# Four pairs of weight slices in seven products for the second batch, and where a fifth pair's weight sums are made

## The chip, the cores and the metric

The kernel runs on one core of a Trainium2 chip. The metric is the device time of one execution in microseconds (us). Three runs of the kernel before gave 648.67, 646.83 and 647.27 us, so a median of 647.27 us.

## The reference

Two stages are computed for 4 batches of 768 tokens. The first is attention of 8 heads of width 64 over chunks of 32 tokens (with 16 tokens of context on the left, 8 on the right and 8 memory tokens). The second is a mixer over the result `x`, cut here to what matters:

```python
h = x.transpose(0, 2, 1) @ U @ V              # over tokens, rank 32
u = x + h.transpose(0, 2, 1)                  # 768 x 512 per batch
ch = np.maximum(u @ w_ch1, 0.0) @ w_ch2       # 512 -> 2048 -> 512
return (u + ch).astype(np.float32)
```

Nearly all of TensorE's time goes into the two products of the last but one line. The kernel keeps each factor of them as a high and a low part (`h` and `l` at the end of a name) and a product is three passes: high by high, low by high, high by low.

## The kernel before

The 2048 hidden columns are 16 slices of 128, numbered f, in 8 pairs p = 0 to 7 (f = 2p and 2p+1). The 768 tokens of a batch are two blocks of 384 (three tiles of 128).

**Batch 0** (`both_blocks`, L1566) works in 32 units. A unit is one slice for one block: `w1_step` (12 matmuls of 384 columns into a PSUM bank `ps_h`), relu and split into `hh` and `hl`, then `w2_step` (9 matmuls of 512 columns into three accumulators). The second block takes its last slices in the order 15, 14, 10, 11, 12, 13, so the last unit, n = 31, is slice 13.

**Batches 1 to 3** (`sevens`, L1304) take a pair of slices and both blocks together. The four products of half slices by half blocks' channels that would be eight are made as seven from sums of weights and sums of `u` (a Strassen form). A product is `six` (L1311): 6 matmuls of 384 columns. The seven run in the order 0 to 6 in the loop from L1399, with copies (`keep`, ScalarE) and additions (`add`, VectorE) of partial results between them. Product 2 and product 4 use the same bank, so product 4 starts only after `keep(c12, xb)`; products 4 and 5 read the sums `t34h`, `t34l` of `u`.

**In batch 1** the first `2 * NPL` = 10 slices (`few`) don't go that way. In the loop at L1374 each slice is two products with the plain weights (`half_of`, `other`), for the first block; its second block follows after the loop over pairs (`other_half`, two products a slice). So five pairs take eight products each (L1355, L1360, L1449) and pairs 5, 6 and 7 take seven.

**Sums of weights.** The sums that products 2, 3, 4 and 6 need are made once per pair, in `take_value` (L511) and `keep_sums` (L487). GpSimd adds high and low part of a slice (`whole`, L485) and makes four sums (L495); ScalarE and VectorE split each into high and low (L498, L499); `save_sums` (L502) writes them to DRAM with four DMAs. The working place is `vbs[1]` (two halves of it are also the home of the first two sums) and two slots, so one pair must be finished with before the next one begins. Pairs 7, 5 and 6 are done at the end of batch 0, pairs 0 to 3 in the loop of L1374, and pair 4 behind `other_half` of slices 8 and 9. The saves of one pair are issued when the next one is taken.

**The ring of weights.** Low parts and sums come from DRAM in items of 256 KB, in the order of `list_items` (L1270), into a ring of 5 tiles `w1l`; `next_item` (L1299) gives out one and asks for the item four ahead. Loads wait for the tile that they overwrite: for the matmuls that read it and, in the plain slices, for `whole` on GpSimd.

**What sets the order.** TensorE and the DMA queue of SyncE (SP) run in the order of the program text. VectorE, ScalarE and GpSimd are ordered by a list scheduler when the kernel is built, except that ScalarE and VectorE keep the text's order among the instructions emitted between L1384 (the last plain slice) and `closing.close()` (L1421, behind the first pair's first split). The attention of the next batch (`attention`, L526) is a generator of 49 pieces, handed out by `pace` (L1648): after call t of `give`, `49 * t // slots` pieces have been emitted. `slots` (L1675) is 47. Piece 14 is `s_part(0)`, the scores of one third of the tokens (L708) with their maximum, subtraction, exponent and sums (L715 to L744); 25 and 33 are the same for the other thirds; 16 and 17 transpose the first third's probabilities (L762), and 19 is `av_part(0)` (L782). The sums of `u` for batch 1 (`seven_u`, L1193) are handed out by `NEXTS` in the last three plain slices; what is left of them, `t34h` and `t34l`, is emitted behind the first pair's first split (L1416).

```python
        product(xb, 0, True)                      # L1408
        ...
        keep(c11, xb)
        even()
        product(yb, 1, True)
        add(c11, yb, c11)
        h1 = split(c11)
        ...
        product(xb, 2, False)                     # L1423
        keep(c12, xb)
        give()
        product(yb, 3, True)
        other_places()
        product(xb, 4, False)
```

In batch 1 `even` and `give` hand out pieces of attention, and `other_places` does nothing. Between the two parts of the quotation, for the first pair alone, lie the rest of `seven_u`, the `w2_step` of the last plain slice and `closing.close()`.

Of the kernel before, what the change touches and what calls it, by code (L numbers as in the profile page):

```python
# [35 lines left out]
SPLIT = 10  # L36
# [5 lines left out]
PACE = 27  # L42
NSOLO = 2
SEVEN = 1
NPL = 5
LASTW = 13
NEXTS = {3: (1, 1), 2: (2, 3), 1: (1, 1)}
RING = 4
# [12 lines left out]
def chunk_attn_then_mixer_kernel(  # L61
# [56 lines left out]
    def w1_home(f, shape, dtype, name):  # L118
        return (w1q if f >= LASTW else w1r if f in (2 * NPL - 2, 2 * NPL - 1) else w1p).tile(shape, dtype, name=name, tag=f"w1_{f}")

# [245 lines left out]
    def save_w1l():  # L366
        while unsaved:
            f, w1l = unsaved.pop(0)
            p, odd = divmod(f, 2)
            for n, w in enumerate((w1h[f], w1l)):  # L370
                if odd:
                    nc.sync.dma_start(out=w1s_d[p][:, 5, n].bitcast(F32), in_=w[:, 2:4].bitcast(F32))
                    if n or p < NPL:
                        nc.sync.dma_start(out=w1x_d[p][:, n].bitcast(F32), in_=w[:, 0:2].bitcast(F32))
# [87 lines left out]
    def advance(n):  # L462
        for _ in range(n):
            next(weights, None)
# [7 lines left out]
    def load_w1l(f, w1l):  # L472
        p, odd = divmod(f, 2)
        if odd:
            nc.sync.dma_start(out=w1l[:, 0:2].bitcast(F32), in_=w1x_d[p][:, 1].bitcast(F32))
            nc.sync.dma_start(out=w1l[:, 2:4].bitcast(F32), in_=w1s_d[p][:, 5, 1].bitcast(F32))
        else:
            nc.sync.dma_start(
                out=w1l.bitcast(F32).rearrange("p (i c) n -> p i c n", i=2), in_=w1s_d[p][:, 0:2, 1].bitcast(F32),
            )  # L480
# [3 lines left out]
    def whole(out, hi, lo):  # L484
        nc.gpsimd.tensor_tensor(out=out, in0=hi.bitcast(F32), in1=lo.bitcast(F32), op=ALU.add)  # L485

    def keep_sums(p, even, odd, homes):  # L487

        half = 2 * P
        a11, a12, a21, a22 = even[:, :half], even[:, half:], odd[:, :half], odd[:, half:]  # L490
        for out, in0, in1, op in (
            (a22, a21, a22, ALU.add), (a21, a11, a21, ALU.subtract),
            (a11, a22, a11, ALU.subtract), (a12, a12, a11, ALU.subtract),
        ):
            nc.gpsimd.tensor_tensor(out=out, in0=in0, in1=in1, op=op)  # L495
        for (i, val), pair in zip(((3, a22), (4, a21), (2, a11), (6, a12)), homes):
            hi, lo = (pair.bitcast(F32R)[:, half * n:half * n + half] for n in range(2))
            nc.scalar.copy(out=hi, in_=val)  # L498
            nc.vector.tensor_tensor(out=lo, in0=val, in1=hi.bitcast(F32), op=ALU.subtract)  # L499
            unkept.append((p, i, pair))  # L500

    def save_sums():  # L502
        for p, i, pair in unkept:
            nc.sync.dma_start(
                out=w1s_d[p][:, i].rearrange("p h c n -> p (h c n)").bitcast(F32), in_=pair.bitcast(F32),
            )
        unkept.clear()
# [3 lines left out]
    def take_value(f, w1l, homes):  # L511

        p, odd = divmod(f, 2)
        values[f] = homes(f % 2)
        whole(values[f], *(w.rearrange("p c n -> p (c n)") for w in (w1h[f], w1l)))
        if 2 * p in values and 2 * p + 1 in values:
            save_sums()
            keep_sums(p, values.pop(2 * p), values.pop(2 * p + 1), [homes(2 + n) for n in range(4)])
# [604 lines left out]
    def more_w():  # L1123
        while loaded[0] < min(NF, done[0] // 2 + EARLY):
            if loaded[0] >= 5 and front[0]:
                return
            if loaded[0] >= LASTF - NDEC and done[0] < ndec[0]:
                return
            load_w(loaded[0])
            loaded[0] += 1  # L1130
# [32 lines left out]
    def turn_x1(c):  # L1163

        ps = att_ps()
        for tt in range(TB):
            nc.tensor.matmul(
                out=ps[:, tt * P:(tt + 1) * P], lhsT=xs[(0, TB + tt)][:, c * P:(c + 1) * P],
                rhs=ident, start=(tt == 0), stop=False, skip_group_check=True,
            )  # L1170
        return ps
# [93 lines left out]
    ring, fetched, used, items = [], [0], [0], []  # L1265

    def others(few):
        return list(range(few - 2, few)) + list(range(few - 2)) if few else []

    def list_items(b):  # L1270

        def whole_item(src):
            def load(w):
                nc.sync.dma_start(
                    out=w.rearrange("p h c n -> p (h c n)").bitcast(F32),
                    in_=src.rearrange("p h c n -> p (h c n)").bitcast(F32),
                )

            return load

        def low_item(f):
            return lambda w: load_w1l(f, w.rearrange("p i c n -> p (i c) n"))

        few = 2 * NPL if b == 1 else 0
        items.extend(low_item(f) for f in range(few))
        items.extend(whole_item(w1s_d[p][:, n]) for p in range(few // 2, NF // 2) for n in range(7))
        for f in others(few):
            p, odd = divmod(f, 2)
            items.append(whole_item(w1x_d[p] if odd else w1s_d[p][:, 0]))
            items.append(whole_item(w1s_d[p][:, 5 if odd else 1]))  # L1290

    def fetch_sums(upto):
        while fetched[0] < min(len(items), upto):
            w = wlo.tile([P, 2, 2, P], F32R, name="w1l")
            items[fetched[0]](w)
            ring.append(w)
            fetched[0] += 1
# [6 lines left out]
    def sevens(b, give, following, last_step=None):  # L1304

        few, closing = 2 * NPL if b == 1 else 0, ExitStack()
        if few:
# [254 lines left out]
    def get_w1l(f):  # L1562
        if f not in w1ls:
            w1ls[f] = fetch_w1l(f)

    def both_blocks():  # L1566

        units = []
        for f in range(SPLIT + LEAD):
            if f < SPLIT:  # L1570
                units.append((0, f, 0, f == 0, None))
            if f >= LEAD:
                g = f - LEAD
                units.append((1, g, 1, g == 0, False if g == SPLIT - 1 else None))
        units += [(0, f, 0, False, True if f == NF - 1 else None) for f in range(SPLIT, NF)]
        order = [NF - 1, NF - 2] + list(range(SPLIT, NF - 2))
        units += [(1, f, 0, f == order[0], True if f == order[-1] else None) for f in order]
        prev, taken = None, [0]
        for n, (blk, f, where, begins, ends) in enumerate(units):
            while done[0] < min(2 * NF, 2 * f + 2):  # L1580
                advance(1)
                more_w()
            if n == 2:
                head.close()
            if n == PACE:
                paced.close()
            for _ in range(SPREAD.get(n, 0)):
                next(spreading)
            for blk_, m, *_ in units[n:n + AHEAD + 3]:
                if SPLIT <= m < NF - 2 and blk_ == 1:  # L1590
                    get_w1l(m)
            if n + RING >= len(units):
                if not items:
                    list_items(1)
                fetch_sums(n + RING + 1 - len(units))
            w1l = w1ls[f]
            if SPLIT <= f < NF - 2 or blk == 1:
                del w1ls[f]
            placed = iter(PLACE.get(n, ()))

            def between():
                upto = next(placed, 0)
                while taken[0] < upto:
                    next(gen[0])
                    taken[0] += 1

            def joins():
                for c, g3 in rest:
                    join_uT1(turn_x1(c), c, g3)
                advance(2)  # L1610

            hid_ = w1_step(0, blk, f, w1l, between if n else joins)
            if blk and f >= 2 * NPL:
                take_value(f, w1l, slot_home if f >= NF - 2 else work_home)
            for _ in range(RATE):
                if n >= 2 * SPLIT or done[0] < 2 * (f + WLO):
                    advance(1)
                more_w()
            between()
            if prev is not None:  # L1620
                while done[0] < 2 * prev[1] + 2:
                    advance(1)
                    more_w()
                w2_step(0, *prev, between)
            between()
            prev = (blk, f, where, begins, ends) + hid_
        return lambda: w2_step(0, *prev)
# [43 lines left out]

    gen[0], coming[0] = attention(1, xs), seven_u(1, fine=True)
    last_step = both_blocks()
    for b in range(1, B):
        slots = 2 * 2 * NPL - 1 + 6 * (NF // 2 - NPL) + 2 + 2 * LATER if b == 1 else 6 * (NF // 2) + LATER  # L1675
        if b == 1:
# [37 lines left out]
```

## Time and profile before

| | before |
|---|---|
| median of three runs | 647.27 us (646.83 to 648.67) |
| the profiled execution, its own time | 647.38 us |
| its span, first to last instruction | 645.6 us |
| TensorE matmul busy | 622.4 us, 96% |
| VectorE, ScalarE, GpSimd busy | 375.4, 255.5, 113.9 us |
| mean granted TensorE clock | 0.994 |

The span starts at 0. Batch 0's last `w2_step` ends at 218.4 us, where batch 1's first product starts; its plain slices run until 265.0 us, its three pairs until 312.4 us, and batch 2 starts at about 373 us. A row of the timeline gives start, duration, engine, line, operation and operands, and in brackets how long the engine stood idle before it and what ended that. Matmuls overlap, so a row's duration is not what a matmul costs: the distance from one row's start to the next one's is.

### The profile page before, as it was taken

How to read it: one execution, taken by the hardware profiler on the slowest of the kernel's cores; microseconds unless marked ns; L12 is line 12 of the kernel's file. 1: busy time of each engine (PE TensorE's matmuls, PEld its weight loads, DVE VectorE, ACT ScalarE, POOL GpSimd, SP SyncE). 2: the span in 40 equal slices, each digit the busy share in tenths (PEclk: the TensorE clock that was granted, in tenths of full speed). 3: DMA queues.
4: the chain of work that ended last, by engine and by line, in shares of the span. 5: the costliest groups of instructions: out<-in, count | busy, mean ns of one | idle time of the engine just before them, and what ended most of it. 6: DMA issues, size and time to landing. Idle time of an engine off the chain costs nothing.

```text
span 645.6 us, 15062 instructions
## 1 busy us (share of the span) xinstructions
PE 622.4 (96%) x6027; PEld 538.6 (83%) x6030; DVE 375.4 (58%) x715; ACT 255.5 (40%) x641; POOL 113.9 (18%) x202
## 2 busy tenths in 40 slices
PE   8788999999899999999999999999999999999997
PEld 5657999988786888788889799998977899999886
DVE  6947788798783837844655835553456732222323
ACT  4525444448332545522255613421347621221221
POOL 4200000043154455100434100000025200000000
PEclk9899999999999999999999999999999999999999
DMA  8994577667897699666489859667423055565201
GB/s 235 170 351 169 178 247 225 229 190 179 179 183 203 158 320 284 198 183 186 140 242 204 164 166 308 202 169 196 119 70 94 1 183 176 147 174 153 97 0 50
DMA packets 168706, 115.03 MB, mean 178 GB/s; under 512 B 100956, under 2 KB 139484, under 8 KB 168636
## 3 DMA queue, kind: packets, MB, share of 16 engines
q1 hardware_dynamic: 168012, 113.92, 63.0%
q8 instruction: 48, 0.79, 0.5%
q10 hardware_dynamic: 624, 0.15, 0.1%
q14 instruction: 22, 0.18, 0.1%
HBM read 90.83 MB, written 28.97 MB: 186 GB/s over the span
## 4 chain that ended last, share of the span: by engine, by line
PE 57%; DVE 5%; ACT 3%; DMA 3%; issue 2%; SPq 1%; POOL 1%; ACTq 0%
PE ps_h L1315 24%; PE acc L1546 16%; PE acc L1556 8%; PE ps_a L782 2%; PE ps_h L1495 2%; ACT uc L171 1%; DMA blocks<-spread 1%; PE acc L1540 1%; DMA w1l<-w1s 1%; SPq L610 1%; PE ps_a L708 1%; PE ps_a L812 1%; PE ps_a L762 1%; DVE x L1511 1%; POOL vb L495 1%
## 5 line engine op out<-in xcount | busy, mean ns | idle before, releaser
L1546 PE MATMUL acc<-w,hh 128*128 128x512 f32 x612 | 157.7, 393 | 1.3 <-ACT hh L1329 1.3
L1546 PEld LDWEIGHTS acc<-w,hh 128*128 128x128 f32 x612 | 113.3, 188 | 22.9 <-ACT hh L1329 2.8
L1556 PE MATMUL acc<-w,hl 128*128 128x512 f32 x306 | 87.0, 393 | 0.0
L1556 PEld LDWEIGHTS acc<-w,hl 128*128 128x128 f32 x306 | 56.8, 188 | 11.8
L1315 PE MATMUL ps_h<-t12h,w1l 128*128 128x384 f32 x192 | 55.7, 343 | 0.6 <-ACT c L1341 0.6
L1315 PE MATMUL ps_h<-bh,w1l 128*128 128x384 f32 x192 | 52.9, 340 | 0.0
L1315 PE MATMUL ps_h<-t34h,w1l 128*128 128x384 f32 x152 | 46.4, 346 | 0.3 <-ACT hst L1341 0.2
L171 POOL COPY uc<-y 32x128 f32<-32x128 f32 x96 | 32.9, 342 | 77.0 <-ACT hh L1329 36.7
L1495 PE MATMUL ps_h<-uh,w1h 128*128 128x384 f32 x124 | 42.5, 347 | 2.2 <-ACT w1h L397 1.2
L1495 PE MATMUL ps_h<-ul,w1h 128*128 128x384 f32 x124 | 41.3, 337 | 0.4 <-DVE ul L1189 0.4
L1330 DVE SCALAR_TENSOR_TENSOR hl<-ps_h,hh 128x384 fp32r<-128x384 f32 x29 | 16.1, 554 | 42.9 <-ACT hh L1329 42.8
L1337 DVE TENSOR_TENSOR c<-ps_h,c 128x384 f32<-128x384 f32 x19 | 10.5, 552 | 51.6 <-PE ps_h L1315 51.6
L1315 PEld LDWEIGHTS ps_h<-t12h,w1l 128*128 128x128 f32 x192 | 35.3, 188 | 3.2 <-ACT c L1341 1.0
L1330 DVE SCALAR_TENSOR_TENSOR hl<-hst,hh 128x384 fp32r<-128x384 f32 x36 | 20.4, 570 | 28.6 <-PE acc L1556 21.3
L1315 PEld LDWEIGHTS ps_h<-bh,w1l 128*128 128x128 f32 x192 | 35.1, 188 | 0.8
L1315 PE MATMUL ps_h<-b,w1l 128*128 128x384 f32 x174 | 35.4, 338 | 0.0
L1329 ACT ACTIVATE hh<-ps_h 128x384 fp32r<-128x384 f32 x29 | 14.2, 491 | 52.3 <-PE ps_h L1315 52.2
L1337 DVE TENSOR_TENSOR hst<-ps_h,hst 128x384 f32<-128x384 f32 x36 | 19.9, 553 | 24.0 <-ACT hst L1341 16.8
L1315 PE MATMUL ps_h<-t12l,w1l 128*128 128x384 f32 x96 | 32.4, 337 | 0.0
L1341 ACT COPY c<-ps_h 128x384 f32<-128x384 f32 x19 | 9.1, 479 | 57.9 <-PE ps_h L1315 57.9
L1329 ACT ACTIVATE hh<-hst 128x384 fp32r<-128x384 f32 x36 | 18.8, 524 | 32.3 <-PE acc L1546 29.8
L1503 ACT ACTIVATE hh<-ps_h 128x384 fp32r<-128x384 f32 x31 | 15.2, 491 | 40.3 <-PE ps_h L1495 40.3
(253 smaller groups left out, 1269.0 us busy)
## 6 DMA issues: line engine op xcount, KB each, us to landing
w1l<-w1s SPq DMA_DIRECT2D x155, 256.0 KB
rw<-in_moe_w_ch_dram SPq DMA_DIRECT2D x14, 512.0 KB
out_dram<-x SPq DMA_DIRECT2D x24, 256.0 KB
blocks<-spread SPq DMA_DIRECT2D x24, 256.0 KB
vb<-in_v_dram SPq DMA_DIRECT2D x56, 98.0 KB
raw<-in_moe_w_ch_dram SPq DMA_DIRECT2D x20, 256.0 KB
rw<-in_moe_w_ch_dram SPq DMA_DIRECT2D x16, 256.0 KB
w1s<-sums SPq DMA_DIRECT2D x16, 256.0 KB
```

The lines of the kernel that those rows point to most:

```text
L171: (nc.scalar.copy if (5 * to + at) % 8 < 3 else nc.gpsimd.tensor_copy)(out=dst[CK * to:CK * to + CK, :, CK * at:CK * at + CK], in_=y[CK * ...
L495: nc.gpsimd.tensor_tensor(out=out, in0=in0, in1=in1, op=op)
L782: nc.tensor.matmul(out=psv[g][CK * i:CK * i + CK, t, j], lhsT=pt[s][rows, 2 * t + k_, CK * i:CK * i + CK], rhs=vt[rows, NI * t + i, D * j: ...
L1315: nc.tensor.matmul(out=ps[:, :TOK], lhsT=w_, rhs=u, start=(start and m == 0), stop=(m == 5), skip_group_check=True,)
L1329: nc.scalar.activation(out=hh, in_=c, func=AF.Relu)
L1330: nc.vector.scalar_tensor_tensor(out=hl, in0=c, scalar=0.0, in1=hh.bitcast(F32), op0=ALU.max, op1=ALU.subtract,)
L1337: nc.vector.tensor_tensor(out=out, in0=ps[:, :TOK], in1=in1, op=ALU.add)
L1341: nc.scalar.copy(out=out, in_=ps[:, :TOK])
L1495: nc.tensor.matmul(out=ph[:, :TOK], lhsT=w[:, c, :], rhs=u[c], start=(m == 0), stop=(m + 1 == len(parts)),)
L1503: nc.scalar.activation(out=hh, in_=ph[:, :TOK], func=AF.Relu)
L1546: nc.tensor.matmul(out=acc[tt], lhsT=h[:, sl], rhs=w, start=(begins and m == 0), stop=False,)
L1556: nc.tensor.matmul(out=acc[tt], lhsT=hl[:, sl], rhs=w2h[f], start=False, stop=ends is not None)
```

## The change

`NPL` becomes 4: slices 0 to 7 are plain, and pair 4 (slices 8 and 9) joins pairs 5, 6 and 7 in seven products. `few` is 8 and `slots` 49. Pair 4's sums are now made at the end of batch 0: its two low parts are the first two items of the ring (`LATE`), taken behind the last unit by `take_value` and not by products, and two further items are asked for at once.

```diff
-NPL = 5
+NPL = 4
+LATE = (8, 9)
@@ list_items
         few = 2 * NPL if b == 1 else 0
+        if few:
+            items.extend(low_item(f) for f in LATE)
         items.extend(low_item(f) for f in range(few))
@@ both_blocks
             hid_ = w1_step(0, blk, f, w1l, between if n else joins)
-            if blk and f >= 2 * NPL:
+            if blk and f >= SPLIT:
                 take_value(f, w1l, slot_home if f >= NF - 2 else work_home)
+            if n + 1 == len(units):
+                for f_ in LATE:
+                    take_value(f_, ring.pop(0).rearrange("p i c n -> p (i c) n"), work_home)
+                used[0] += len(LATE)
+                fetch_sums(used[0] + RING)
```

`SPLIT` is 10, so the second condition stands for the same slices as before.

## Rows read from the trace of the kernel before

**Rows 1.** The page: the span, and each engine's busy time.
```profile
span 645.6 us, 15062 instructions
...
PE 622.4 (96%) x6027; PEld 538.6 (83%) x6030; DVE 375.4 (58%) x715; ACT 255.5 (40%) x641; POOL 113.9 (18%) x202
```

**Rows 2.** TensorE's waits, 218 to 312 us: total, times, longest.
```profile
PE ps_h L1315 <- ACT hst L1341: 0.7, 3, 0.3
PE ps_h L1315 <- ACT c L1341: 0.6, 1, 0.6
PE ps_h L1315 <- DVE hl L1330: 0.5, 1, 0.5
PE ps_a L782 <- ACT pT L765: 0.3, 1, 0.3
```

**Rows 3.** Timeline of TensorE, batch 1, plain slices and first pairs.
```profile
224.16 0.44 PE L1315 MATMUL ps_h<-bh,w1h 128*128 128x384 f32 x1 [0.49 <-DVE hl L1330]
...
253.31 1.51 PE L708 MATMUL ps_a<-kall,qt 64*32 64x64 f32 x128
...
273.71 0.45 PE L1315 MATMUL ps_h<-t34h,w1l 128*128 128x384 f32 x1 [0.18 <-ACT hst L1341]
...
275.21 1.55 PE L1546 MATMUL acc<-w,hh 128*128 128x512 f32 x6
...
277.27 0.34 PE L1315 MATMUL ps_h<-t34h,w1l 128*128 128x384 f32 x1
...
278.32 1.22 PE L1315 MATMUL ps_h<-b,w1l 128*128 128x384 f32 x6
279.38 1.52 PE L1546 MATMUL acc<-w,hh 128*128 128x512 f32 x6
280.83 1.48 PE L708 MATMUL ps_a<-kall,qt 64*32 64x64 f32 x128
...
285.97 0.44 PE L1315 MATMUL ps_h<-t12h,w1l 128*128 128x384 f32 x1 [0.63 <-ACT c L1341]
```

**Rows 4.** Timeline of SP's queue around the end of batch 0.
```profile
213.51 0.37 SPq L478 DMA_DIRECT2D w1l<-w1s  x1
...
222.69 0.32 SPq L475 DMA_DIRECT2D w1l<-w1x  x1
...
223.58 0.86 SPq L504 DMA_DIRECT2D w1s<-vb  x2
```

**Rows 5.** Timeline of GpSimd at the same place: pair 0's sums.
```profile
212.68 1.30 POOL L485 TENSOR_TENSOR vb<-w1h,w1l 128x512 f32<-128x512 f32 x1 [7.11 <-DVE vb L499]
...
215.23 1.69 POOL L485 TENSOR_TENSOR vb<-w1h,w1l 128x512 f32<-128x512 f32 x1 [0.36 <-DVE sums L499]
217.00 3.04 POOL L495 TENSOR_TENSOR vb<-vb 128x256 f32<-128x256 f32 x3
```

**Rows 6.** Timeline of VectorE: end of batch 0, then the pairs.
```profile
213.40 1.75 DVE L499 TENSOR_TENSOR sums<-vb,sums 128x256 fp32r<-128x256 f32 x2 [0.80 <-ACT sums L498]
...
223.57 1.23 DVE L1330 SCALAR_TENSOR_TENSOR hl<-ps_h,hh 128x384 fp32r<-128x384 f32 x2
...
272.28 1.90 DVE L1197 TENSOR_TENSOR t34l<-tb,t34h 128x512 fp32r<-128x512 f32 x3
...
282.34 1.29 DVE L730 TENSOR_REDUCE mx<-ps_a 128x8 f32<-128x512 f32 x2 [2.20 <-PE ps_a L708]
...
286.68 0.49 DVE L1337 TENSOR_TENSOR c<-ps_h,c 128x384 f32<-128x384 f32 x1
```

**Rows 7.** Timeline of ScalarE: a cast of pair 0, then the first pair.
```profile
226.16 0.41 ACT L498 CAST vb<-vb 128x256 fp32r<-128x256 f32 x1 [0.17 <-DMA w1s<-vb]
...
271.64 1.65 ACT L1217 CAST t34h<-tb 128x512 fp32r<-128x512 f32 x3
273.20 0.46 ACT L1341 COPY hst<-ps_h 128x384 f32<-128x384 f32 x1
```

**Rows 8.** VectorE's splitting of sums, whole span: duration ns min/median/max.
```profile
L499 DVE TENSOR_TENSOR vb<-vb x12: 411/424/1534, 193.7 to 256.6; 128x256 fp32r<-128x256 f32 x12
```

## The prediction

> **What bounds the kernel now.** I read the page first, then TensorE's waits in batch 1, then the timelines of the engines around the places that the change touches. The page shows TensorE busy for 622.4 of 645.6 us [rows 1]; no other engine comes near. In the stretch that the change rewrites TensorE hardly waits: the four largest groups of its waits there come to 2.1 us over 94 us [rows 2]. So TensorE's work sets the time here, a matmul less is worth its cadence, and a wait that VectorE, ScalarE or a transfer puts in front of TensorE costs its whole length. The profiled execution took 647.38 us, 1.78 us more than its span, and the median of the runs is 0.11 us below it; I make the sum against 647.38 and take 0.11 off. I count a change of over 0.3%, some 1.9 us, as one that a measurement can tell from none.
>
> **The change, part by part.**
>
> *Matmuls removed.* Pair 4 takes seven products for eight, so six matmuls of 384 columns go. A product takes from 278.32 to 279.38, 1.06 us [rows 3]. Everything else that TensorE does for slices 8 and 9 stays (the second layer, attention). Term: -1.06 us. That is all that the change removes from the bound.
>
> *Sums of weights moved.* Pair 4's sums (two `whole`, four sums, four casts, four subtractions, four saves) leave the second half of batch 1, where pair 3's take their place, and one pair fewer is made in the plain slices. At the end of batch 0 nothing is added to the pile so much as shifted: what GpSimd does there now for pair 0, from 212.68 to 220.04 [rows 5], it does for pair 4, and pairs 0, 1 and 2 move one place back. GpSimd stays off TensorE's path: its work is hidden behind the last unit and the plain slices. I cost it at nothing, with two exceptions.
>
> The first is VectorE. TensorE already waits 0.49 us at 224.16 for `hl` of slice 0 [rows 3], since VectorE reaches it only at 223.57 [rows 6]. Two of pair 0's casts now run at 226.16 and after, held by a DMA that saves pair 6 [rows 7]. That save stands on SP at 223.58, behind a load that itself waits for TensorE [rows 4]. In the changed text it stands ahead of that load, so pair 4's casts are free by about 220, and their two subtractions, 0.42 us each [rows 8], can land in front of the `hl` that TensorE waits for. Bounds: nothing, if the list scheduler puts them behind, and +0.84 us; I take the middle, +0.4 us.
>
> Here the trace shows more: the same subtraction has a longest of 1534 ns against a median of 424 [rows 8], and a `whole` took 1.69 us against 1.30 for the one before it while VectorE ran its subtractions of 1.75 us for two [rows 5, 6]. The Trainium skill, "SBUF — State Buffer", in its account of the doors, says why: a VectorE operation with two SBUF inputs and a GpSimd operation that reads SBUF take a shared port as an exclusive lock, and the loser waits for the whole of the other instruction. By that rule this move, which sets such subtractions beside GpSimd's sums, would cost more than their medians. The price of that stands with the rivals.
>
> The second is SP's queue, which keeps the text's order. Two loads, of slices 2 and 3, now stand behind the four saves of pair 6, and these wait for pair 6's subtractions, which end at 215.15 [rows 6]. Two saves take 0.86 us to issue [rows 4], four some 1.8; with the load itself about 0.4, slice 2 is on its way by 217.4. The save that began to issue at 223.58 had landed when the cast at 226.16 began, 2.6 us later [rows 4, 7]. By 220 the weights are there, and TensorE wants them at 224.16: 4 us to spare, so nothing. The load for slice 3 also waits for `whole` of slice 8, in the place of today's `whole` that ends at 216.92 [rows 5], and is wanted four microseconds later still. The load for slice 5 waits for slice 0 on TensorE today, until 222.69 [rows 4], and will wait for slice 0's `whole` too, which follows GpSimd's work that ends at 220.04: about a microsecond later, with SP's queue behind it (saves, the output, attention's loads); it is wanted 13 us later. Pair 4's own sums are saved about 225 and read 30 us later. Nothing.
>
> *The first pair's start.* The last plain slice is now slice 7, and by the division in `pace` piece 14 of attention, the scores and softmax of the first third, falls into slice 7 before and after. Before, that was at 253.31, two slices ahead of the first pair [rows 3]. Now it is inside the stretch where ScalarE and VectorE keep the text's order, right ahead of the first pair's copies. The second third shows what that chain takes on VectorE: from 282.34, when L708 ended, to the addition that followed it at 286.68, 4.34 us [rows 6]. Let X be the end of L708. VectorE is free at X + 4.3; then one half-size subtraction of `seven_u` (0.4, an estimate from 1.90 us for three of 128x512), the addition into `c11` (0.5), ScalarE's relu (0.5), the three casts of `t34h` (1.65) and `keep(c12)` (0.46) [rows 6, 7] make X + 7.8. TensorE needs: a third of a `w2_step`, which as a whole goes from 275.21 to 277.27, so 0.69; products 0 and 1, 2.12; the `w2_step` of slice 7, 2.06; products 2 and 3, 2.12: it wants product 4 at X + 7.0. With hand-overs of some 0.2 us in all, it waits 1.0 us, where it waits 0.18 at 273.71 now [rows 3]. Bounds: nothing more, if the scheduler puts `keep(c12)` ahead of the casts, and twice as much, if VectorE comes late to the chain. I take +0.8 us.
>
> *Other pieces of attention.* `slots` goes from 47 to 49 for 49 pieces, so the pieces fall elsewhere among the products. The 0.3 us wait of `av_part(0)` [rows 2] goes: that piece now lies behind product 6 of the first pair, well after its transpositions. The wait of 0.63 us at 285.97, for a copy that stands behind the second third's exponents [rows 2, 3], goes too: L708 ran at 280.83 inside the last `w2_step` of the pair, and now lies ahead of that `w2_step`, with 1.4 us more between it and the next pair. Term: -0.9 us; bounds 0 and -0.9. The scores of the last third move from behind product 2 to between products 0 and 1 of pair 7, where the addition into `c11`, on which product 3 waits, can come behind the softmax. At worst that is 4.34 us of chain less two products, 2.2 us; at best nothing, since the addition has the higher priority. I take +0.3, near the lower end, as the only place like it in these rows, 285.97, cost 0.63 us.
>
> *Behind the pairs* batch 1 has two `other_half` fewer, and between the last of them and batch 2 the same number of second layers and two more. The transpositions of batch 2 that fill that stretch have as long as before. Batches 2 and 3 only shift. Nothing.
>
> Sum: -1.06 + 0.4 + 0.8 - 0.9 + 0.3 = -0.46 us. From 647.38 that is 646.9, against the median 646.8 us.
>
> **The rivals.**
>
> *All covers hold* (faster). The list scheduler puts pair 4's subtractions and `keep(c12)` where they hurt nobody, and the last third's scores too: -1.06 - 0.9 - 0.18 = -2.1 us, so 645.1 us. For it: the additions and copies on TensorE's path have a high priority. Against it: the first pair's instructions keep the text's order, and there the arithmetic above is tight. Chance 0.2.
>
> *The ring runs dry at slice 2* (slower). It has one place: the load of slice 2 behind the saves of pair 6. Were pair 6's subtractions to end as late as pair 0's do, with the sums until 220.04 [rows 5] and a cast and a subtraction of 0.4 each after them, the saves would be issued at 222.7, the load at 223.1, and the weights land at 225.7 or, with a transfer twice as long, 228.3. TensorE would stand 1.6 to 4.2 us longer; with 2.9 the time is 649.7 us. The point that decides is an issue by 221.6, 2.6 us ahead of 224.16. For it: SP stood from about 214 to 222.69 behind one load of this ring [rows 4]. Against it: the row that ends at 215.15. Chance 0.1. A wait on slots or on the first softmax, of a similar size, I add with 0.05.
>
> *The shared port* (a little slower). One subtraction of the two at the end of batch 0 takes 1.53 us for 0.42 and another pair's the same, each ahead of something that TensorE waits for: +2.2 less the 0.4 already counted, so 648.6 us. The rule of the skill gives this as the result of the move; the trace has it at its longest only [rows 8]. Chance 0.1.
>
> *The change does less than it says:* that the six matmuls go is sure, since no other instruction takes their place on TensorE; if the waits that I strike out stay, the time is 647.7 us. That is inside my forecast.
>
> **How the numbers follow.** The forecast, a gain of about one microsecond in which waits old and new nearly cancel, has 0.55; its own range is 645.9 to 647.8 us. With the rivals at 0.2, 0.15 and 0.1 the range that holds 8 in 10 reaches from 644.9, just past the case in which all covers hold, to 648.9, past the port and into the ring's case. Faster by over 0.3% is the first rival, with a tail of the forecast: 0.21. Slower by over 0.3% is the ring with its like: 0.14. Within 0.3%: 0.65.
>
> **What would show it.** Right: TensorE's matmuls fall by six; the first product of pair 4 comes near 254.5 to 257; a wait of about 1 us ahead of product 4 of that pair, put down to a ScalarE copy; no wait of 0.6 us at the start of pair 6; SP's saves of pair 6 near 215. Wrong: a wait at slice 2 or 3 put down to a DMA of `w1l`; a wait for VectorE at slice 2 well over 1.3 us; idle time in batches 2 or 3 that was not there before, which nothing here foresees.

## The result, and the profile after

The changed kernel takes 657.67 us (median of 4 runs, 655.30 to 658.94) against 647.05 us for the kernel before (4 runs): a ratio of 1.0137 with an interval of 1.0107 to 1.0168. By that ratio it is slower by about 9 us (the two medians lie 10.6 us apart); the forecast was 646.8, its range ended at 648.9. The profiled execution took 658.94 us, 1.84 more than its span. Line numbers of the changed kernel are up to three higher than before: L1318 is the L1315 of [rows 3], L499 the L498 of [rows 7].

From the page of the changed kernel, as in [rows 1]:
```profile
span 657.1 us, 15068 instructions
...
PE 625.8 (95%) x6021; PEld 541.6 (82%) x6024; DVE 376.3 (57%) x716; ACT 256.0 (39%) x642; POOL 113.3 (17%) x202
```
The six matmuls are gone (6027 to 6021), and yet TensorE is busy for 3.4 us longer. The span grew by 11.5 us, so the other 8 us are idle time.

TensorE's waits from 219 to 283 us (total, times, longest), the answer to [rows 2]:
```profile
PE ps_h L1318 <- ACT bh L1218: 3.4, 1, 3.4
PE ps_h L1318 <- DVE bl L1198: 1.8, 1, 1.8
PE ps_h L1318 <- ACT hst L1344: 1.8, 1, 1.8
PE ps_h L1318 <- ACT t34h L1218: 1.1, 1, 1.1
PE ps_h L1318 <- DVE t34l L1198: 1.0, 1, 1.0
```
These are the five largest, 9.1 us in all; the kernel before has none of this length there. On TensorE's timeline they stand at four places, the first two together:
```profile
218.73 0.84 PE L1559 MATMUL acc<-w,hl 128*128 128x512 f32 x3
222.96 0.44 PE L1318 MATMUL ps_h<-bh,w1h 128*128 128x384 f32 x1 [3.39 <-ACT bh L1218]
225.24 0.69 PE L1318 MATMUL ps_h<-bl,w1h 128*128 128x384 f32 x1 [1.84 <-DVE bl L1198]
...
254.06 0.45 PE L1318 MATMUL ps_h<-bh,w1h 128*128 128x384 f32 x1 [1.78 <-ACT hst L1344]
...
273.57 0.45 PE L1318 MATMUL ps_h<-t34h,w1l 128*128 128x384 f32 x1 [1.06 <-ACT t34h L1218]
275.06 0.45 PE L1318 MATMUL ps_h<-t34l,w1l 128*128 128x384 f32 x1 [1.05 <-DVE t34l L1198]
```

**The first place is slice 0 itself.** Batch 0's last second layer ends at about 219.5, and the first half of slice 0 (`half_of(0)`) cannot begin, since `bh` isn't there. ScalarE makes it, in three parts, of which the first came at 214.63; this is what ScalarE did after that, in the changed kernel:
```profile
215.87 0.41 ACT L499 CAST vb<-vb 128x256 fp32r<-128x256 f32 x1 [0.22 <-POOL vb L496]
218.81 0.41 ACT L499 CAST vb<-vb 128x256 fp32r<-128x256 f32 x1 [2.53 <-POOL vb L496]
219.63 0.40 ACT L499 CAST sums<-vb 128x256 fp32r<-128x256 f32 x1 [0.41 <-POOL vb L496]
220.49 0.41 ACT L499 CAST sums<-vb 128x256 fp32r<-128x256 f32 x1 [0.46 <-POOL vb L496]
220.81 1.06 ACT L1214 COPY uc<-ps_a 128x512 f32<-128x512 f32 x2
221.76 1.15 ACT L1218 CAST bh<-uc 128x512 fp32r<-128x512 f32 x2
```
and in the kernel before, from the same place:
```profile
215.78 0.59 ACT L1213 COPY uc<-ps_a 128x512 f32<-128x512 f32 x1
216.40 0.62 ACT L1217 CAST bh<-uc 128x512 fp32r<-128x512 f32 x1
219.25 0.41 ACT L498 CAST sums<-vb 128x256 fp32r<-128x256 f32 x1 [2.23 <-POOL vb L495]
220.06 0.41 ACT L498 CAST sums<-vb 128x256 fp32r<-128x256 f32 x1 [0.41 <-POOL vb L495]
```
Both kernels have casts that wait for GpSimd's sums, and both show an idle ScalarE for over 2 us in front of one. Before, the last `uc` and `bh` of batch 1 had gone ahead, so the idle time cost nothing. Now all four casts of pair 4 stand ahead of the last two `uc` and `bh`, and these start 5.5 to 6.7 us later (about 1 us of that is batch 0, whose last second layer ends that much later in this execution). The Trainium skill, "PSUM — Partial Sum Buffer", section "Engine vs sequencer instructions", says that the queues of ScalarE, VectorE and GpSimd are strictly first in, first out. The trace agrees: ScalarE stood idle for 2.53 us in front of a cast while the copy behind it, whose transposition TensorE had done by 216.8, was not taken until 220.81.

VectorE has the same order. Its timeline in the changed kernel, with the four subtractions of pair 4 (L500; the third, at 220.40, is among the lines left out) ahead of the `bl` of slice 0:
```profile
217.11 1.06 DVE L500 TENSOR_TENSOR vb<-vb 128x256 fp32r<-128x256 f32 x1
219.25 0.63 DVE L500 TENSOR_TENSOR vb<-vb 128x256 fp32r<-128x256 f32 x1 [1.07 <-ACT vb L499]
...
221.93 0.41 DVE L500 TENSOR_TENSOR sums<-vb,sums 128x256 fp32r<-128x256 f32 x1
222.42 2.77 DVE L1198 TENSOR_TENSOR bl<-uc,bh 128x512 fp32r<-128x512 f32 x2
```

**Behind these waits the clock falls** in this execution. Windows of the changed kernel: stretch, its length, busy time and instructions of TensorE's matmuls, its weight loads, VectorE, ScalarE and GpSimd, then the granted clock, the DMA share and GB/s.
```profile
225.20:228.20 3.00, 2.96 (x10) 2.96 (x10) 0.14 (x1) 0.78 (x2) 2.03 (x3) 0.52 0.02 5
...
255.70:259.70 4.00, 4.00 (x15) 3.64 (x15) 3.61 (x8) 2.19 (x5) 1.50 (x3) 0.61 0.72 164
...
276.80:279.50 2.70, 2.70 (x9) 2.18 (x9) 0.56 (x1) 0.67 (x2) 0.00 (x0) 0.54 0.33 97
```
At 0.52 TensorE is close to its lower level of 1.2 GHz for nearly the whole stretch. What a stretch loses is its length times what is missing to 1: 3.0 x 0.48 = 1.4 us, 4.0 x 0.39 = 1.6 us, 2.7 x 0.46 = 1.2 us, and 0.5 more for the stretch of 1.8 us ahead of the last one, at 0.74. That is 4.7 us, and it explains why six matmuls fewer are busy for longer. Waits (9.1) and clock (4.7) less the six matmuls (1.06) and the waits of [rows 2] (2.1) make 10.7 us of the 11.5.

**The second place, 254.06,** is the second half of slice 6, which goes on in a bank that a ScalarE copy (`hst`) has to read first. A part of it comes through loads on SP's queue. SP's queue in the changed kernel, as in [rows 4]:
```profile
212.67 1.25 SPq L505 DMA_DIRECT2D w1s<-vb  x2
215.27 1.20 SPq L505 DMA_DIRECT2D w1s<-sums  x2
216.56 0.38 SPq L479 DMA_DIRECT2D w1l<-w1s  x1
...
230.54 0.32 SPq L476 DMA_DIRECT2D w1l<-w1x  x1
...
245.26 0.94 SPq L537 DMA_DIRECT2D blocks<-spread  x2
```
The saves of pair 6 and slice 2's load go out as predicted. The load for slice 5, which waits for slice 0 on TensorE, goes at 230.54 for 222.69 [rows 4], in both kernels 1.3 us after the second half of slice 0 begins on TensorE (229.25 and 221.41), and all that stands behind it on SP is late as well: two `blocks` of attention go from 245.26 on, where before they went from 237.84 on. VectorE transposes the second of them from 251.43 on, 6.2 us after the two began to issue, where it took 5.1 us before (237.84 to 242.9). ScalarE's copies of `kall` wait for that transposition, and they stand ahead of the `hst` copy that slice 6's second half needs. VectorE's and ScalarE's rows:
```profile
251.43 0.71 DVE L647 STREAM_TRANSPOSE kall<-blocks 128x512 f32<-128x512 f32 x1 [1.98 <-DMA blocks<-spread]
252.18 0.38 ACT L648 COPY kall<-kall 128x224 f32<-128x224 f32 x1 [1.34 <-DVE kall L647]
...
253.53 0.48 ACT L1344 COPY hst<-ps_h 128x384 f32<-128x384 f32 x1
```
The kernel before has such copies of `kall` ahead of `hst` here too, and waits 0.21 us for it (245.01). Lateness alone does not make the difference: these loads go 7.4 us later than before, but TensorE is 7.8 us late as well since slice 0. What is new is that the second load took 1.1 us longer from issue to transposition, and that a copy `uc` (0.57 us at 253.06) now stands ahead of `hst`. No run separates the two, and the wait is not fixed: without the text's order (below) the changed kernel has 0.79 us here behind the same waits at slice 0.

### The profile page after: what moved, and what is told of

Read it like the earlier page. It is cut to its first block, busy times and chain, and to the rows that moved or that the text cites. A ratio compares the mean times of both kernels' runs of the same rounds, so it can differ in the third digit from the quotient of the medians.

```text
span 657.1 us, 15068 instructions
## 1 busy us (share of the span) xinstructions
PE 625.8 (95%) x6021; PEld 541.6 (82%) x6024; DVE 376.3 (57%) x716; ACT 256.0 (39%) x642; POOL 113.3 (17%) x202
## 4 chain that ended last, share of the span: by engine, by line
PE 71%; DVE 9%; DMA 7%; ACT 5%; issue 3%; SPq 2%; POOL 2%; ACTq 0%; POOLq 0%; DVEq 0%
PE ps_h L1318 25%; PE acc L1549 20%; PE acc L1559 10%; PE ps_h L1498 6%; PE ps_a L783 2%; DMA rw<-in_moe_w_ch_dram 2%; PE acc L1543 1%; PE ps_a L1549 1%; PE ps_a L709 1%; PE ps_a L763 1%; DVE vb L261 1%; DMA blocks<-spread 1%; ACT uc L172 1%; PE ps_a L813 1%; DVE mx L731 1%
## 5 line engine op out<-in xcount | busy, mean ns | idle before, releaser
L1549 PEld LDWEIGHTS acc<-w,hh 128*128 128x128 f32 x612 | 114.7, 190 | 22.9 <-ACT hh L1332 2.2
L1318 PE MATMUL ps_h<-t12h,w1l 128*128 128x384 f32 x192 | 56.1, 345 | 0.3 <-DVE c L1340 0.3
L1318 PE MATMUL ps_h<-bh,w1l 128*128 128x384 f32 x192 | 54.0, 344 | 0.0
L1318 PE MATMUL ps_h<-t34h,w1l 128*128 128x384 f32 x160 | 49.0, 347 | 1.3 <-ACT t34h L1218 1.1
L1318 PEld LDWEIGHTS ps_h<-t12h,w1l 128*128 128x128 f32 x192 | 35.2, 188 | 3.2 <-issue 1.1
L1318 PEld LDWEIGHTS ps_h<-bh,w1l 128*128 128x128 f32 x192 | 35.8, 191 | 0.9
L1318 PE MATMUL ps_h<-b,w1l 128*128 128x384 f32 x168 | 34.2, 339 | 0.0
L1332 ACT ACTIVATE hh<-ps_h 128x384 fp32r<-128x384 f32 x28 | 13.7, 491 | 51.9 <-PE ps_h L1318 51.8
L1318 PE MATMUL ps_h<-t12l,w1l 128*128 128x384 f32 x96 | 32.3, 337 | 0.0
L1318 PEld LDWEIGHTS ps_h<-t34h,w1l 128*128 128x128 f32 x160 | 29.5, 188 | 3.2 <-ACT t34h L1218 1.4
```

The source lines that it names most:

```text
L1318: nc.tensor.matmul(out=ps[:, :TOK], lhsT=w_, rhs=u, start=(start and m == 0), stop=(m == 5), skip_group_check=True,)
L1332: nc.scalar.activation(out=hh, in_=c, func=AF.Relu)
L1549: nc.tensor.matmul(out=acc[tt], lhsT=h[:, sl], rhs=w, start=(begins and m == 0), stop=False,)
```

## The experiments

All ratios are to the kernel before, run on the same chip beside the experiment; on these chips its median was 648.7 to 649.1 us. My theory, called A: the casts and subtractions of pair 4's sums, placed early in ScalarE's and VectorE's queues, hold up slice 0's copies behind them. The rivals: the sums cost through GpSimd's work itself or through memory traffic, wherever they are placed; B, SP's queue is late, and all transfers behind it; or C, the loss is the seven products' own, with pair 4 pulled into the stretch where ScalarE and VectorE keep the order of the text.

**Pair 4's casts on GpSimd.** If the casts on ScalarE alone were the block, this removes it.
```diff
-            nc.scalar.copy(out=hi, in_=val)
+            (nc.gpsimd.tensor_copy if 2 * p in LATE else nc.scalar.copy)(out=hi, in_=val)
```


> The changed kernel with pair 4's four casts to high parts on GpSimd, not ScalarE. Theory A (ScalarE's queue: these casts stand ahead of the copies uc and bh that batch 1's first product needs, and wait for GpSimd's sums): the waits of 3.4 and 1.8 us at batch 1's first product go, with the slow clock behind them; 648 to 651 us. Theory B (SP's queue: the load of slice 5 waits for GpSimd's addition, and all transfers behind it come late): GpSimd gets longer by four casts, so the load is later still; 657 us or more. Theory C (the first pair's product 4, waiting behind the softmax, with the clock that falls after it): no change, 656 to 658 us.

655.71 us, ratio 1.0098 (1.0065 to 1.0131): still slow. ScalarE's, VectorE's and TensorE's timelines, in this order:
```profile
214.52 1.15 ACT L1218 CAST bh<-uc 128x512 fp32r<-128x512 f32 x2
...
218.81 0.61 DVE L500 TENSOR_TENSOR sums<-vb,sums 128x256 fp32r<-128x256 f32 x1
219.34 1.76 DVE L1198 TENSOR_TENSOR bl<-uc,bh 128x512 fp32r<-128x512 f32 x1
...
221.36 0.68 DVE L1198 TENSOR_TENSOR bl<-uc,bh 128x512 fp32r<-128x512 f32 x1
...
222.09 0.69 PE L1318 MATMUL ps_h<-bl,w1h 128*128 128x384 f32 x1 [5.13 <-DVE bl L1198]
```
`bh` is ready by 215.7 and the wait for ScalarE is gone, but TensorE waits 5.13 us for `bl` instead. VectorE's subtractions were the second block of the same kind, hidden behind the first; in this run they wait for GpSimd, which now makes the casts too. Theory A had named one queue where there are two; as I had stated it, with ScalarE as the one to blame, it fell, and it stands in the wider form. Whoever frees one engine of two that wait for the same thing gains little.

**Pair 4's sums left out.** The seven products stay; the late block and its loads go, and pair 4 reads pair 5's sums in place of its own. What is left out is all the work of making pair 4's sums.
```diff
-            items.extend(low_item(f) for f in LATE)
...
-whole_item(w1s_d[p][:, n])
+whole_item(w1s_d[5 if p == 4 else p][:, n])
...
-                for f_ in LATE:
-                    take_value(f_, ring.pop(0).rearrange("p i c n -> p (i c) n"), work_home)
```


> The changed kernel without pair 4's sums of weights: the two early ring items, the additions, casts, subtractions and saves are left out, and pair 4's products use pair 5's weight sums, so the output is not the reference's. The seven products of pair 4 stay. Theory A and theory B: both expect 647 to 650 us, since the casts are gone and SP's order is the old one; at batch 1's start TensorE waits as little as before. Theory C: 655 to 658 us. The forecast's sum for the seven products alone (six matmuls fewer, product 4's wait) would be 646 to 648 us.

649.18 us, ratio 0.9998 (0.9982 to 1.0014). The whole loss is gone with the sums. TensorE's waits from 212 to 312 us:
```profile
PE ps_h L1316 <- ACT c L1342: 1.1, 1, 1.1
PE ps_h L1316 <- DVE t34l L1198: 1.0, 1, 1.0
PE ps_h L1316 <- ACT t34h L1218: 1.0, 1, 1.0
PE ps_h L1316 <- DVE hl L1331: 0.5, 1, 0.5
```
No wait at slice 0, and SP's load for slice 5 goes at 221.58. Product 4's two waits are the ones of the changed kernel, so they belong to the seven products. The gain of six matmuls is given back there, and the rest of my sum, no measurable change, is what this kernel does. The rival that puts the loss on the seven products falls.

**The sums moved alone.** The kernel before, with five pairs of plain slices and eight products for pair 4, but pair 4's sums made at the end of batch 0:
```diff
+LATE = (8, 9)
...
+            items.extend(low_item(f) for f in LATE)
...
-                if f + 2 >= few:
+                if f + 2 >= few and f not in LATE:
...
-            if f + 1 == few:
+            if f + 1 == few and f not in LATE:
...
+            if n + 1 == len(units):
+                for f_ in LATE:
+                    take_value(f_, ring.pop(0).rearrange("p i c n -> p (i c) n"), work_home)
```


> The kernel before with one part of the change: five pairs stay plain, but pair 4's sums are made at the end of batch 0 and no longer in the second half of batch 1. Theory A: the same order on ScalarE as in the changed kernel, so the wait of 5 us at batch 1's first product is there, with a slow clock behind it; 652 to 656 us. Theory B: the same, 652 to 656 us, but then the wait is named after a DMA. Theory C: 646.5 to 648 us.

654.12 us, ratio 1.0086 (1.0055 to 1.0117). The waits of slice 0 and the one for `hst` are there, without the seven products:
```profile
PE ps_h L1318 <- ACT bh L1218: 3.5, 1, 3.5
PE ps_h L1318 <- DVE bl L1198: 1.8, 1, 1.8
PE ps_h L1318 <- ACT hst L1344: 1.4, 2, 1.2
```
and the clock behind them:
```profile
222.20:226.20 4.00, 3.75 (x12) 3.75 (x13) 0.62 (x2) 0.78 (x2) 2.25 (x3) 0.50 0.02 4
```
The two runs together show the cause from both sides: the sums without the seven products are slow, the seven products without the sums are not. They don't add up, though: 0.9% and nothing against 1.4% together. The wait for `hst` is at slice 6 and 1.8 us in the changed kernel, with a slow clock behind it; here the longer one is at slice 4 and 1.2 us, and the clock is at 1.00 in the 4 us behind it. I did not separate these some 3 us further.

**The sums emitted later.** The same block, moved to the end of the unit's text. The same work is done by the same engines; only its place in their order changes, which is what theory A is about.
```diff
-            if n + 1 == len(units):
-                for f_ in LATE:
...
             prev = (blk, f, where, begins, ends) + hid_
+            if n + 1 == len(units):
+                for f_ in LATE:
...
```
(The block stands ahead of `prev`.)

> The changed kernel with the block that takes pair 4 moved to the end of the last unit in the text, behind the copies uc, bh and bl of batch 1; the list scheduler then puts only one of the four casts and one of the four subtractions ahead of the last bh and bl. Theory A (batch 1's first product waits because the casts and subtractions of pair 4, which wait for GpSimd's sums, stand ahead of bh and bl on ScalarE and VectorE): the wait of 5 us falls to 1 us or less, the slow clock behind it goes, and the wait of 1.8 us at slice 6 falls with it; 0 to 3 us above the kernel before, as without the sums. Theory B (SP's queue is late): SP's order is nearly the same, so 6 us or more above the kernel before.

654.03 us (10 runs), ratio 1.0064 (1.0039 to 1.0089). TensorE's first product of slice 0, and ScalarE ahead of it:
```profile
217.73 0.34 PE L1318 MATMUL ps_h<-bh,w1h 128*128 128x384 f32 x1
218.84 0.45 PE L1318 MATMUL ps_h<-bl,w1h 128*128 128x384 f32 x1 [0.77 <-DVE bl L1198]
...
225.16 0.44 PE L1318 MATMUL ps_h<-bh,w1h 128*128 128x384 f32 x1 [1.33 <-DVE hl L1333]
```
```profile
215.77 0.62 ACT L1218 CAST bh<-uc 128x512 fp32r<-128x512 f32 x1
217.12 0.41 ACT L499 CAST vb<-vb 128x256 fp32r<-128x256 f32 x1 [0.73 <-POOL vb L496]
218.26 0.41 ACT L499 CAST sums<-vb 128x256 fp32r<-128x256 f32 x1 [0.73 <-POOL vb L496]
```
Three of the casts now stand behind the last `bh`, and 5.2 us of waiting at slice 0 have become 0.77: the order was it, since the work is the same. This settles where the wait at slice 0 comes from. The time came back only by half: A had expected 0 to 3 us above the kernel before, B 6 or more, and it is 4 to 5. In the profile 1.33 us stay at slice 0's `hl`, 0.49 before [rows 3], and later 1.6 us for a copy of `c`, 0.9 for `hst` and product 4's 2.1.

**Attention's pieces two ahead.** Product 4 waits for the chain of the first softmax, so let that run earlier, with the sums where the change has them:
```diff
-pace(slots, 4 if b == 2 else 0)
+pace(slots, 4 if b == 2 else -2 if b == 1 else 0)
```


> The changed kernel with attention's pieces handed out two earlier in batch 1, so that the first third's scores and softmax come in slice 6 and not right ahead of the first pair. Theory C: the waits of 1.1 and 1.0 us at product 4 go, and the slow clock behind them; if they are the main loss the time falls to about 650 us. Theory A: at most 2 to 4 us are gained (653.5 to 656 us), and the wait of 5 us at batch 1's first product stays. Theory B: no change within 1 us.

656.20 us, ratio 1.0123 (1.0094 to 1.0151): no better. Product 4's waits are gone, but three new ones took their place: 1.4 us at L709 put down to issue, 1.3 for a transfer of `w1l`, 0.9 for a softmax. The two edits together (later sums and earlier pieces):

> The kernel of the run sums_emitted_later with attention's pieces two earlier in batch 1. Theory A with C for what is left: the waits of 1.0 and 1.0 us at product 4 go, but waits of the kind that pieces_two_ahead brought (0.9 for probabilities, 1.3 for a load, 1.4 at L709) may take their place; 2 us below to 1 us above sums_emitted_later.

652.97 us, ratio 1.0076 (1.0048 to 1.0104), no different from the later sums alone: the softmax wait at L763 grew to 3.0 us. Moving this chain moves its wait.

**No text order for the first pairs.** The line that keeps ScalarE and VectorE to the text's order in that stretch goes, in four kernels:
```diff
-                    closing.enter_context(tc.manual_schedule(engines=CLOSING))
+                    pass
```
With the sums emitted later:

> The kernel of the run sums_emitted_later without the stretch in which ScalarE and VectorE keep the text's order; the list scheduler then puts the casts of t34h ahead of the copy of c11 and of the softmax's exponents. If product 4 waits for the text's order, its waits of 1.0 and 1.0 us go, and the time is 1 to 3 us below sums_emitted_later; if it waits for VectorE's load as such, they stay, or come back as a wait for c11 or for the split of it, and the time is the same within 1 us.

646.82 us, ratio 0.9983 (0.9954 to 1.0013). The remaining loss is gone, and product 4's waits with it; `hl` (1.3), `bl` (0.9) and `hst` (0.7) stay. Then in the kernel before, in the changed one, and in the one without pair 4's sums (leaving out the same as above):

> The kernel before without the stretch in which ScalarE and VectorE keep the text's order. If the text's order costs only where the softmax falls into it (its scores lay two slices ahead here), the time is the kernel before's within 2 us; if it costs as such, it is 3 us or more below the kernel before, and the gain of later_no_text_order has nothing to do with the seven products.

> The changed kernel, pair 4's block in its place, without the stretch of text order. Theory A: the wait of 5 us at batch 1's first product and the slow clock behind it stay, so some 5 us above the kernel before; the waits of 1.1 and 1.0 us at product 4 go. If both losses add up, the time lies 3 to 6 us below the changed kernel's.

> The changed kernel without pair 4's sums (left out; its products use pair 5's, so the output is not the reference's) and without the stretch of text order: what six matmuls fewer are worth when neither loss is there. By the forecast's sum 1 to 2 us below the kernel before; by the waits that no_sums_of_pair4 had at product 4 (2.1 us and the slow clock behind them) 2 to 4 us below no_sums_of_pair4.

Before: 646.54 us, ratio 0.9968 (0.9945 to 0.9992). Changed: 654.20, 1.0086 (1.0061 to 1.0111); its waits for `bh` (3.4) and `bl` (1.8) are untouched. Without the sums: 646.31, 0.9964 (0.9937 to 0.9990). So the text's order costs about 0.3% in the kernel before too, which I had not expected, and without it the picture is the same: seven products alone, nothing that can be told (0.9964 against 0.9968); with the sums where the change puts them, 1.2% more. The kernel with the sums emitted later and no text order was measured a second time, in more rounds, to tell whether it beats the kernel before:

> The kernel of the run later_no_text_order once more, with more rounds: 0 to 2.5 us below the kernel before; whether it beats the kernel before is what this run is for.

648.34 us, ratio 0.9991 (0.9967 to 1.0014): it doesn't. Of the kernels that compute the reference's output, only the kernel before without its text order has an interval below 1, by 0.3%, and it ends just short of 1; that it beats the kernel with later sums and no text order is not shown, since their intervals overlap.

## Why the prediction was wrong

It was wrong in sign and size, and above all by one step. "**Sums of weights moved**" said that what GpSimd does for pair 0 it now does for pair 4, and: "I cost it at nothing, with two exceptions". The two exceptions stood at slice 2's weights and at `hl` of slice 0. The loss began ahead of both, at the first product of slice 0, with 5.23 us of waits and some 1.4 us of slow clock. Against the kernel without the sums the sums cost 1.39%, some 9 us, where I had +0.4.

What failed in that step can be named exactly. I treated pair 4's work as if it took pair 0's place in every queue, and checked GpSimd (covered, rightly) and VectorE at one later point. I read ScalarE only from 226.16 on [rows 7], where two of pair 0's casts run. The two casts ahead of these, at 219.25 and 220.06, I left out, and in front of the first ScalarE stood idle for 2.23 us, waiting for GpSimd. A waiting cast is a closed door in a queue: harmless where it stands, and worth 5 us if it stands a few instructions earlier. Pair 0's sums come later in the text than the last copies of batch 1, pair 4's come ahead of them. The diff shows that, and I didn't ask who stands behind the moved instructions on each engine. The bound of +0.84 us was wrong with it: it counted the subtractions' own duration and not what they wait for.

*Matmuls removed*: right, 6027 to 6021. Pair 4's first product came at 265.57, not at 254.5 to 257, because of the waits and the clock ahead of it; without the sums it came at 253.59.

*SP's queue*: right at slice 2. The saves of pair 6 were issued at 212.67 and 215.27, slice 2's load from 216.56, and no wait for `w1l` came. The rival of the ring that runs dry did not happen. The load for slice 5 went 7.9 us later, not about one, since it waits for TensorE. That the queue behind it may be late at no cost did not hold quite: the loads of `blocks` behind it have a part in the 1.78 us at 254.06.

*`hl` of slice 0*: 0.20 us in the changed kernel, since all of it came later. Where slice 0 starts on time, in the run with the sums emitted later, it is 1.33 against 0.49: +0.84, the upper bound of the term, for 0.4 taken.

*The first pair's start*: the place was right, a ScalarE instruction ahead of product 4, and the first of the two waits is 1.06 us for the 1.0 computed. That the size agrees is luck:
```profile
271.07 0.48 ACT L1344 COPY hst<-ps_h 128x384 f32<-128x384 f32 x1 [1.40 <-PE ps_h L1318]
...
271.87 1.65 ACT L1218 CAST t34h<-tb 128x512 fp32r<-128x512 f32 x3
```
The sum had `keep(c12)` behind the casts of `t34h`. It ran ahead of them (the `hst` at 271.07), the case for which the lower bound said "nothing more", and product 4 waits for the casts themselves. They end 8.7 us behind the scores (L709, until 264.83), where the sum without `keep(c12)` makes 7.35, and TensorE wants product 4 at 7.7, not 7.0. And the term stopped at `t34h`. The subtraction has a wait of its own of 1.05 us, to which VectorE's transposition of `kall` (0.70 us at 273.73) between the second and the third `t34l` adds, and a slower clock behind it costs another 1.7 us. So the term is some 3.6 us (1.06 + 1.05 + 1.7, less the 0.18 that was there) for 0.8 in the changed kernel. The waits are the same without the sums, where the clock is at 0.74 and 0.69 in the two stretches of 3 us that hold and follow them.

*Other pieces of attention*: the 0.3 us of `av_part(0)` and the 0.63 us at pair 6 are gone, as said; the last third's scores cost no more than a wait of 0.3.

*The shared port*: it is seen, on other instructions than the rival's. Of the last two `bl` of slice 0 one took 1.79 us beside an addition on GpSimd; with the casts on GpSimd it was 1.76 beside an addition from 219.11 on, and 0.68 for the next, which began while GpSimd stood idle. The Trainium skill, "SBUF — State Buffer", section "SBUF: two separate sides", has this as an exclusive lock, and the trace agrees, at some 1.1 us an instruction. It is a part of the 1.84 us wait and no more, and not a new one: before, the two took 2.48 us together (216.14), and 2.77 after. Of the rival's own subtractions one took 1.06 us, the other three 0.63, 0.41 and 0.41, and its time, 648.6, was not the result. The row that I read for it was misread: the `whole` of 1.69 us began at 215.23, when the subtractions had ended (215.15) [rows 5, 6]; beside it ran a `bl`, from 215.07.

## What to carry to other kernels

When work is moved to an earlier place, list for each engine that it uses what it waits for and what stands behind it there; the duration of the moved instructions is the smallest part of their price. An idle time "until" another engine on a queue off the critical path is a marked door: note which instructions have passed it, and whether the change puts it ahead of them. And make the experiment that moves the same work a few instructions on, before the one that moves it to another engine: here the second only uncovered the next queue.

## What was not expected of the hardware

A wait of a few microseconds on TensorE can cost more than its length. In the profiled execution of the changed kernel the granted clock was 0.52 over 3.0 us after TensorE had stood for 3.39 and 1.84 us; after 1.78 us it was 0.61 over 4.0 us; after 1.06 and 1.05 us it was 0.74 over 1.8 and 0.54 over 2.7 us: 1.4 to 1.7 us more at each place. In the kernel without pair 4's sums a single wait of 1.11 us at 259.03 left the clock at 1.00 in the 3 us around it, and two of 1.04 and 1.05 us in a row did not.

It is not a fixed price. With the sums emitted later, product 4 has the same two waits of 1.06 and 1.05 us, 4 us behind one of 1.63, and the clock stayed at 1.00 (columns as above; it is 1.00 in the 7 us that follow, too):
```profile
264.00:268.00 4.00, 1.89 (x10) 1.32 (x9) 3.23 (x6) 3.81 (x12) 0.00 (x0) 1.00 0.63 192
```
Single waits of 1.55 us (246.45, pieces two ahead) and 1.64 us (252.11, casts on GpSimd) left it at 1.00 in the 4 us behind them. And a kernel's executions differ: the profiled one with the sums emitted later took 651.54 us at a mean clock of 1.00, while the median of its ten runs was 654.03 us and their mean clocks went down to 0.991. So a part of what that kernel did not get back may be clock; no profile shows it.
